# Interleaving the units of the first two token blocks, and giving the eight PSUM banks roles

## The chip, the cores and the metric

One core of a Trainium2 chip runs the whole program. The metric is the device time of one execution in microseconds (us). The core has a matrix engine (TensorE, PE in the profile; its weight loads are PEld), a vector engine (VectorE, DVE), a scalar engine for activations (ScalarE, ACT), a general engine (GpSimd, POOL) and a queue engine that issues most DMA transfers (SyncE, SP). Each engine works through its own instructions strictly in order, and waits on semaphores for the others.

## The reference

Three stages follow one another on 4,608 tokens of 512 features. Only the shapes and the formulas matter here.

```python
# q, k, v: (8 batches, 8 heads, 576, 64)
q_s = softmax(q, axis=-1)            # exp(q - max) / sum, over the 64
k_s = softmax(k, axis=2)             # over the 576 positions
kv  = einsum('bhsd,bhse->bhde', k_s, v)
x   = einsum('bhsd,bhde->bhse', q_s, kv)     # reordered to (4608, 512)

h = x @ w_in                          # (512, 2048)
x = (h * cos(h)) @ w_out              # (2048, 512)

# a token with x @ w_skip > 0 goes through one of 8 experts (argmax of x @ w_gate)
x + gate * (relu(x @ w1[e]) @ w2[e])
```

`w_in` and `w_out` arrive as 64-bit floats, 16.8 MB together, and are turned into 32-bit parts on the chip.

## The kernel before, in words

**Blocks and units.** The tokens are cut into 12 blocks of 384. The hidden width of 2,048 is cut into 16 chunks of 128. A *unit* `n` is one block and one chunk, block = n // 16, chunk = n % 16, so the blocks come one after another. A unit is: `h_mm` (line 318), 12 matmuls of 384 columns into one PSUM bank of the three of pool `ps_h`; the chain `chain_a`, `chain_b`, `chain_c` (lines 326 to 342), which computes h cos(h) by ACT and DVE in turn and splits it into a high and a low part, the low part by POOL (line 342); and `out_mm` (line 344), 9 matmuls of 512 columns into three banks `o0` to `o2`, which collect the output of a block over its 16 chunks. Every product is made of three (high x high, high x low, low x high). The last reader of an `h` bank is the operation of line 335, at the end of `chain_b`.

**The loop.** Iteration n (line 927) issues `h_mm(n)`, then `chain_b(n-1)`, `chain_a(n)`, `chain_c(n-1)`, then `out_mm(n-3)` (LAG is 3). After the last chunk of a block, `evac` (line 356) copies the three `o` banks out: bank 0 and 2 by ACT, bank 1 by DVE (line 361). Between these, numbers in tables say at which chunk other work is issued:

- `attention(j)` makes the input of block j while block j-1 is worked on: `kmax_a`, `kmax_b`, `kmax_c`, `k_exp`, `kv_mm` for a new batch, `q_max`, `q_exp`, `q_norm` for the block's q, then `q_trans` and `x_make`, which leave `xT[j]`, the operand of `h_mm`. `q_max` subtracts on POOL (line 247), `q_norm` multiplies on POOL (line 261). From block 2 on q is transposed by 16 DMAs (`reblock`, line 275) and four DVE operations (`turn`); for blocks 0 and 1 by TensorE.
- `routing(j)` takes the output of block j to the choice of an expert, while block j+1 is worked on.
- `w_step` (line 163): a step turns one 128x512 weight into two 32-bit words (lines 148, 149, 154, 155), finishes the weight of two steps before (lines 143, 152; line 152 on POOL for the weights named in `LOP`, else on DVE), and issues the load of the weight seven steps on. There are 32 weights, two to a chunk. In block 0 the tables `WA`, `WB`, `WC` spread the steps, as every chunk of block 0 needs two new weights.

```python
            w_turn(order[t] if t < len(order) else None, order[t - 2] if 2 <= t < len(order) + 2 else None)
...
            if n < N:
                h_mm(n)
            if 0 <= n - 1 < N:
                chain_b(n - 1)
            if n < N:
                chain_a(n)
            if 0 <= n - 1 < N:
                chain_c(n - 1)
```

**The head and the end.** Before the first unit (lines 873 to 925) come the loads, the attention of block 0 in two halves, the first three weight steps, and matmuls on zeros (`warm`). After the last block come tiles of 256 tokens of one expert (`compute`), at most one tile of 128 (`small`, behind a branch for each of two parities, line 1015), and tiles of 64 (`tiny`, line 676). `tiny` makes all 512 hidden values of a half in one bank `ph`, then four times relu, transpose and copy (lines 697 to 699), then the output matmuls (line 705).

**PSUM.** Eight banks: three `o`, three `h`, two `m` (`misc`, for everything else, among it the attention and the routing).

## Time and profile before

| | |
|---|---|
| three runs | 1260.59, 1261.05, 1454.27 us; median 1261.05 |
| the profiled execution, device time | 1259.9 us |
| its span, first to last recorded event | 1258.1 us |
| mean granted clock of PE | 0.983 of full speed |

The profile is of one execution; its span leaves 1.8 us of the device time outside. A row of a window or a group gives busy time in us and, in brackets, a count of instructions. PEclk is the clock that PE was granted as a share of 2.4 GHz; its lower level is 1.2 GHz. In a group of operations the last part names what ended the idle time before them.

### The profile page before, as it was taken

The page shows a single profiled execution, that of the slowest core. Times are in us where ns is not written, and L with a number is a line of the kernel's source. Part 1 is how long each engine was busy: PE and PEld are TensorE (multiplying, and loading weights), DVE is VectorE, ACT ScalarE, POOL GpSimd, SP SyncE. Part 2 cuts the span into 40 slices and gives each one's busy share as a digit, 9 for nine tenths or more (in the row PEclk, how much of TensorE's full clock was granted, in tenths as well). Part 3 has the DMA queues.
Part 4 walks back from the last instruction along what each step waited for, and adds up shares of the span by engine and source line. Part 5 has one row for each costly group of instructions (what it writes and reads, how often), then busy time and mean ns, then how long its engine had stood idle before and what let it go on. Part 6 is the DMA issues. An engine that isn't in the chain of part 4 may idle for free. (4 is left out here: it accounts for less than half of the span.)

```text
span 1258.1 us, 19774 instructions
## 1 busy us (share of the span) xinstructions
PE 1205.7 (96%) x7012; PEld 1059.3 (84%) x7012; DVE 754.0 (60%) x1508; ACT 719.7 (57%) x1395; POOL 410.8 (33%) x365
## 2 busy tenths in 40 slices
PE   7778999999999999999999999999999999999986
PEld 4657898888898888989988888988888889999974
DVE  7999735556354555635454554535575976776751
ACT  3667655655666565566655566565575545545541
POOL 3666532334324233432423333242120222131121
PEclk8988999999999999999999999999999999999998
DMA  9920222234212223421323232221054677677653
GB/s 301 369 82 1 59 39 68 51 64 111 53 58 44 76 52 64 111 44 49 60 51 79 64 101 35 67 53 25 26 168 160 178 250 230 213 236 229 212 171 107
DMA packets 209493, 138.75 MB, mean 110 GB/s; under 512 B 138200, under 2 KB 173272, under 8 KB 209376
## 3 DMA queue, kind: packets, MB, share of 16 engines
q1 hardware_dynamic: 204272, 125.13, 36.2%
q0 software_dynamic: 5104, 12.17, 2.8%
q8 instruction: 60, 0.98, 0.3%
q14 instruction: 57, 0.47, 0.1%
HBM read 106.35 MB, written 15.95 MB: 97 GB/s over the span
## 5 line engine op out<-in xcount | busy, mean ns | idle before, releaser
L323 PE MATMUL h<-xh,w 128*128 128x384 f32 x1536 | 435.2, 345 | 22.0 <-POOL w L152 6.6
L351 PE MATMUL o<-w,gh 128*128 128x512 f32 x1152 | 364.4, 397 | 2.5 <-ACT x L363 2.5
L323 PEld LDWEIGHTS h<-xh,w 128*128 128x128 f32 x1536 | 283.9, 190 | 39.7 <-DVE w L152 7.7
L342 POOL TENSOR_TENSOR gl<-a,gh 128x384 fp32r<-128x384 f32 x176 | 184.9, 1051 | 395.1 <-ACT gh L340 289.5
L323 PE MATMUL h<-xl,w 128*128 128x384 f32 x768 | 261.4, 340 | 0.1
L351 PEld LDWEIGHTS o<-w,gh 128*128 128x128 f32 x1152 | 215.2, 189 | 39.6 <-ACT x L363 4.1
L351 PE MATMUL o<-w,gl 128*128 128x512 f32 x576 | 229.5, 399 | 1.6 <-POOL gl L342 1.6
L335 DVE SCALAR_TENSOR_TENSOR a<-a,h 128x384 f32<-128x384 f32 x192 | 104.6, 545 | 191.9 <-ACT a L334 191.9
L328 ACT ACTIVATE a<-h 128x384 f32<-128x384 f32 x192 | 93.1, 485 | 182.0 <-PE h L323 107.8
L329 DVE SCALAR_TENSOR_TENSOR a<-a,h 128x384 f32<-128x384 f32 x192 | 105.3, 549 | 140.0 <-ACT a L328 139.9
L323 PEld LDWEIGHTS h<-xl,w 128*128 128x128 f32 x768 | 146.0, 190 | 5.6 <-DVE xl L314 0.7
L340 ACT CAST gh<-a 128x384 fp32r<-128x384 f32 x192 | 97.9, 510 | 72.4 <-DVE a L335 72.4
L844 PE MATMUL h<-xh,w 128*128 128x256 f32 x704 | 137.5, 280 | 0.3 <-DVE w L123 0.3
L351 PEld LDWEIGHTS o<-w,gl 128*128 128x128 f32 x576 | 108.9, 189 | 29.6 <-POOL gl L342 2.8
L123 DVE TENSOR_TENSOR w<-wr,w 128x512 fp32r<-128x512 f32 x192 | 123.9, 687 | 8.1 <-ACT w L122 2.5
L844 PEld LDWEIGHTS h<-xh,w 128*128 128x128 f32 x704 | 113.3, 189 | 4.1 <-ACT w L122 0.7
L855 PE MATMUL o<-w,gh 128*128 128x512 f32 x352 | 112.9, 401 | 0.0
L122 ACT CAST w<-wr 128x512 fp32r<-128x512 f32 x192 | 108.7, 619 | 1.9 <-DMA wr<-in_w 1.9
L333 ACT ACTIVATE a<-a 128x384 f32<-128x384 f32 x192 | 100.8, 525 | 11.0 <-DVE a L329 10.7
L334 ACT ACTIVATE a<-a 128x384 f32<-128x384 f32 x192 | 100.8, 525 | 6.1
L847 ACT ACTIVATE gh<-h 128x256 fp32r<-128x256 f32 x88 | 33.7, 384 | 120.3 <-PE h L844 96.7
L844 PE MATMUL h<-xl,w 128*128 128x256 f32 x352 | 98.7, 280 | 0.0
(220 smaller groups left out, 1470.7 us busy)
## 6 DMA issues: line engine op xcount, KB each, us to landing
wr<-in_w SPq DMA_DIRECT2D x101, 512.0 KB, 4.4
qt<-in_q SPq DMA_DIRECT2D x12, 768.0 KB, 6.7
out<-x SPq DMA_DIRECT2D x36, 256.0 KB, 2.2
wr<-in_w_in SPq DMA_DIRECT2D x16, 512.0 KB, 9.9
wr<-in_w_out SPq DMA_DIRECT2D x16, 512.0 KB, 11.1
xl<-x SPq DMA_DIRECT2D x160, 48.0 KB, 2.1
xh<-qt SPq DMA_DIRECT2D x160, 48.0 KB, 2.1
vt<-in_v SPq DMA_DIRECT2D x7, 1040.0 KB, 6.5
```

The lines of the kernel that those rows point to most:

```text
L122: nc.scalar.copy(hi, src)
L123: nc.vector.tensor_tensor(lo, src, hi.bitcast(F32), op=ALU.subtract)
L323: nc.tensor.matmul(Hp[n], win(a, kk, c), xT[j][b][:, kk, :], start=t == 0, stop=t == len(seq) - 1)
L329: nc.vector.scalar_tensor_tensor(a, a, MAGIC, Hp[n], op0=ALU.subtract, op1=ALU.subtract)
L333: nc.scalar.activation(a, a, AF.Sin, scale=PI)
L334: nc.scalar.activation(a, a, AF.Square)
L335: nc.vector.scalar_tensor_tensor(a, a, 0.5, Hp.pop(n), op0=ALU.subtract, op1=ALU.mult)
L340: nc.scalar.copy(G[n]["h"], a)
L342: eng.tensor_tensor(G[n]["l"], a, G[n]["h"].bitcast(F32), op=ALU.subtract)
L351: nc.tensor.matmul(O[j][g], gg[a][:, g * P:(g + 1) * P], wout(b, c), start=c == 0 and t == 0, stop=c == NC - 1 and t == 2)
L844: nc.tensor.matmul(ps, win2(a, kk, c0, c * P, P), xt[b][:, kk, 0:T2], start=t == 0, stop=t == len(seq) - 1)
L855: nc.tensor.matmul(o[g], g_[a][:, g * P:(g + 1) * P], wout(b, c0 + c), start=c == 0 and t == 0, stop=c == NF - 1 and t == 2)
```

## The change

The units no longer come block by block. A list `UNITS` gives first the chunks 0 to 5 of block 0 (HEAD is 6), then in turn a chunk of block 1 and one of block 0 until block 0 ends (unit 25), then the last six of block 1 (units 26 to 31), then the other blocks as before. The attention of block 1 (`attention_head`) is issued within the iterations 0 to 5, that of block 2 within 8 to 30. The weight steps are one or two an iteration (`WS`), then one, so that they last until iteration 25.

While both blocks are open, both need three `o` banks; so one pool holds all eight banks, and `roles` says which are `o`, `h` and `m`: 3, 3 and 2 up to unit 5, then 3 (block 0) and 3 (block 1) with two `h` and no `m` from unit 6, and again 3, 3 and 2 when block 0 has left its banks, in iteration 28.

The order up to the first unit is another one, with `warm` in portions of four. The subtraction of `q_max` and half of the multiplication of `q_norm` move from POOL to DVE for blocks 0 and 1. The routing of block 0 moves into block 2, beside that of block 1, and its transposition from 16 DMAs and DVE to TensorE (`x2_trans`). `tiny` works in two halves of 256 hidden values with a bank each, and the two branches of `small` change places.

```diff
-WA = (1, 1, 0, 1, 0, 0, 0, 0, 0, 1, 1, 1, 1, 1, 1, 0)
...
+HEAD = 6
+UNITS = [(0, c) for c in range(HEAD)]
+for _c in range(NC - HEAD):
+    UNITS += [(1, _c), (0, HEAD + _c)]
+UNITS += [(1, _c) for _c in range(NC - HEAD, NC)]
+UNITS += [(_j, _c) for _j in range(2, NB) for _c in range(NC)]
...
+KQ = 12, 2, 2
+WS = (1, 1, 2, 2, 2, 2, 2)
...
-    ps_o = m1.enter_context(tc.tile_pool(name="ps_o", bufs=1, space=PSUM))
-    ps_h = m1.enter_context(tc.tile_pool(name="ps_h", bufs=3, space=PSUM))
-    ps_m = m1.enter_context(tc.tile_pool(name="ps_m", bufs=2, space=PSUM))
+    pp = m1.enter_context(tc.tile_pool(name="pp", bufs=1, space=PSUM))
+    banks, used = {}, {"h": 0, "m": 0}
+    def turn_of(kind):
+        used[kind] += 1
+        return bank(banks[kind][used[kind] % len(banks[kind])])
+    roles((0, 1, 2), (3, 4, 5), (6, 7))
...
     def q_max(j, part=None):
...
+            eng = nc.gpsimd if j > 1 else nc.vector
+            eng.tensor_tensor(t, t, st.pop("qm")[:, :, None].to_broadcast([P, NG * H, D]), op=ALU.subtract)
...
+            eng = nc.gpsimd if j > 1 or i else nc.vector
+            eng.tensor_tensor(qt[j][:, :, r, :], qt[j][:, :, r, :],
...
     def attention_head():
+        for c in range(1, 5):
+            add(0, kmax_a, 1, 0, NP, (c,))
+        add(0, q_max, 1)
+        add(1, kmax_b, 1)
+        add(1, x_new, 1)
+        add(1, kmax_c, 1)
+        add(2, q_exp, 1)
+        add(2, k_exp, 1)
+        add(3, q_norm, 1)
+        add(3, kv_mm, 1)
+        for t in range(2):
+            for i in (2 * t, 2 * t + 1):
+                add(4, q_trans, 1, i)
+            for i in (2 * t, 2 * t + 1):
+                add(4 + t, x_make, 1, i)
+        add(KQ[0] - 4, load_q, 2)
+        add(KQ[0], q_max, 2)
+        add(KQ[0] + 1, q_exp, 2)
+        add(KQ[0] + 2, q_norm, 2)
+        add(KQ[0] + 4, q_block, 2)
+        add(KQ[0] + 8, q_turn, 2)
+        add(LAST0, x_new, 2)
+        at = LAST0 + LAG
+        for i in range(NP):
+            add(at + i // 2, q_trans, 2, i)
+            add(at + 1 + i // 2, x_make, 2, i)
+        add(at + 2, x2_trans, 0, 0)
...
-            ph = ps_h.tile([P, DM], F32, tag="h", name="h")
+            ph = [hidden()[:, 0:HM] for v in range(2)]
+            for v, kk in [(0, 0), (1, 0)] + [(v, kk) for v in range(2) for kk in range(1, KD)]:
...
-            for c in range(KD):
-                r = slice(c * P, (c + 1) * P)
-                nc.scalar.activation(a[:, r], ph[:, r], AF.Relu)
-                nc.tensor.transpose(pt[:, r], a[:, r], ident)
-                nc.vector.tensor_copy(g[:, r], pt[:, r])
+            for v in range(2):
+                nc.scalar.activation(a, ph[v], AF.Relu)
+                for c in range(2):
+                    nc.tensor.transpose(pt[:, c * P:(c + 1) * P], a[:, c * P:(c + 1) * P], ident)
+                nc.vector.tensor_copy(g[:, v * HM:(v + 1) * HM], pt)
...
+            if n == POS[1, 0]:
+                roles((5, 6, 7), (3, 4), ())
...
+                if co == NC - 1:
+                    evac(jo, xp)
+                    if jo == 0:
+                        roles((5, 6, 7), (3, 4, 0), (1, 2))
+            if at[0] < len(order) + 2:
+                w_step(WS[n] if n < len(WS) else 1)
...
-        for par, cnt in enumerate((n0, n1) if NE % 2 == 0 else (n1, n0)):
+        for par, cnt in ((1, n1 if NE % 2 == 0 else n0), (0, n0 if NE % 2 == 0 else n1)):
```

**DVE, around `kmax_a`.** The DVE order before, from the chain of units 4 and 5 on; `a` is the chain's tile, `u`, `wr`, `w` belong to the weight step, `km` to the maximum over k.

```order
L335 SCALAR_TENSOR_TENSOR a<-a,h 128x384
L329 SCALAR_TENSOR_TENSOR a<-a,h 128x384
L149 TENSOR_SCALAR u<-wr 128x512
L154 SCALAR_TENSOR_TENSOR wr<-wr,u 128x512
L200 TENSOR_TENSOR km<-kt 128x512
L200 TENSOR_TENSOR km<-km,kt 128x512 x2
L335 SCALAR_TENSOR_TENSOR a<-a,h 128x384
L329 SCALAR_TENSOR_TENSOR a<-a,h 128x384
L149 TENSOR_SCALAR u<-wr 128x512
```

The same engine after the change, from the first chain of unit 0 on; `b_...` is a PSUM bank, `qt` the block's q.

```order
L367 SCALAR_TENSOR_TENSOR a<-a,b_355 128x384
L170 TENSOR_SCALAR u<-wr 128x512
L175 SCALAR_TENSOR_TENSOR wr<-wr,u 128x512
L226 TENSOR_TENSOR km<-kt 128x512
L226 TENSOR_TENSOR km<-km,kt 128x512 x2
L226 TENSOR_TENSOR km<-km,kt 64x512
L274 TENSOR_REDUCE qm<-qt 128x24
L277 TENSOR_TENSOR qt<-qt,qm 128x1536
L373 SCALAR_TENSOR_TENSOR a<-a,b_355 128x384
L367 SCALAR_TENSOR_TENSOR a<-a,b_395 128x384
L170 TENSOR_SCALAR u<-wr 128x512
L173 TENSOR_TENSOR w<-u,w 128x512
```

The maximum over block 1's k starts four units earlier and stands in one piece, and the maximum of q and the subtraction (`qt<-qt,qm`) follow it on DVE.

**PE, two units.** The PE order before, from the last matmul of unit 32 to the first two of unit 33; `h_...` are tiles of the pool of three.

```order
L323 MATMUL h_1970<-xh_1401,w_347 128x384
L351 MATMUL o0_1442<-w_1216,gh_1879 128x512 x2
L351 MATMUL o0_1442<-w_1216,gl_1880 128x512
L351 MATMUL o1_1443<-w_1216,gh_1879 128x512 x2
L351 MATMUL o1_1443<-w_1216,gl_1880 128x512
L351 MATMUL o2_1444<-w_1216,gh_1879 128x512 x2
L351 MATMUL o2_1444<-w_1216,gl_1880 128x512
L323 MATMUL h_2006<-xh_1401,w_385 128x384
L323 MATMUL h_2006<-xl_1402,w_385 128x384
```

After the change, from the last matmul of unit 28 to the first two of unit 29; `b4` is PSUM bank 4, `b0` to `b2` are block 0's output.

```order
L361 MATMUL b4_1714<-xh_435,w_1259 128x384
L389 MATMUL b0_513<-w_1636,gh_1669 128x512 x2
L389 MATMUL b0_513<-w_1636,gl_1670 128x512
L389 MATMUL b1_514<-w_1636,gh_1669 128x512 x2
L389 MATMUL b1_514<-w_1636,gl_1670 128x512
L389 MATMUL b2_515<-w_1636,gh_1669 128x512 x2
L389 MATMUL b2_515<-w_1636,gl_1670 128x512
L361 MATMUL b4_1761<-xh_435,w_1357 128x384
L361 MATMUL b4_1761<-xl_436,w_1357 128x384
```

Unit 29 writes the bank that unit 28 has just written: the list of `h` banks grows from two to three between them, and the turn falls on bank 4 twice.

**PE, one `tiny`.** Before:

```order
L1018 COMPARE_AND_BRANCH
L681 MATMUL m<-ident,tx 128x128 x2
L688 MATMUL h<-wr,a 64x512 x8
L698 MATMUL m<-ident,ta 128x128 x4
L705 MATMUL o<-rv,tg 64x256 x2
L705 MATMUL o<-rx,tg 64x256 x2
L705 MATMUL o<-rv,tg 64x256 x2
L705 MATMUL o<-rx,tg 64x256 x2
L705 MATMUL o<-rv,tg 64x256 x4
L705 MATMUL o<-wr,tg 64x256 x4
```

And after the change, with `b_17806` and `b_17807` the two halves of the hidden values:

```order
L1106 COMPARE_AND_BRANCH
L750 MATMUL b_17801<-ident,tx 128x128 x2
L757 MATMUL b_17806<-wr,a 64x256 x2
L757 MATMUL b_17807<-wr,a 64x256 x2
L757 MATMUL b_17806<-wr,a 64x256 x6
L757 MATMUL b_17807<-wr,a 64x256 x6
L767 MATMUL b_17837<-ident,a 128x128 x2
L767 MATMUL b_17843<-ident,a 128x128 x2
L774 MATMUL b_17847<-rv,tg 64x256 x4
L774 MATMUL b_17847<-rx,tg 64x256 x4
L774 MATMUL b_17847<-rv,tg 64x256 x4
L774 MATMUL b_17847<-wr,tg 64x256 x4
```

The eight matmuls of 512 columns have become sixteen of 256 in two banks, and four transposes in turn have become two pairs.

## Rows read from the trace of the kernel before

**Rows 1.** Page, engines and 40 slices: busy time, then tenths busy per slice

```profile
PE 1205.7 (96%) x7012; PEld 1059.3 (84%) x7012; DVE 754.0 (60%) x1508; ACT 719.7 (57%) x1395; POOL 410.8 (33%) x365
PE   7778999999999999999999999999999999999986
```

**Rows 2.** Windows of DVE-bound and steady stretches: PE, PEld, DVE, ACT, POOL busy, PEclk, DMA

```profile
32.90:66.20 33.30, 21.95 (x99) 18.38 (x98) 31.43 (x42) 18.91 (x39) 21.08 (x17) 0.93 1.06 371
66.20:92.00 25.80, 22.16 (x98) 18.60 (x98) 25.34 (x34) 18.01 (x36) 18.18 (x15) 0.89 0.16 49
92.00:141.50 49.50, 39.73 (x254) 34.52 (x255) 46.58 (x63) 34.88 (x65) 36.06 (x28) 0.90 0.06 17
...
151.10:226.00 74.90, 73.72 (x376) 65.25 (x374) 35.44 (x77) 41.75 (x81) 25.12 (x22) 1.00 0.26 59
...
375.00:447.70 72.70, 72.70 (x373) 64.86 (x372) 35.13 (x77) 41.75 (x80) 24.97 (x22) 1.00 0.27 60
```

**Rows 3.** Waits of PE, 32 to 140 us: total, times, longest

```profile
PE h L323 <- POOL w L152: 6.6, 2, 5.7
PE h L323 <- DVE a L335: 6.0, 3, 2.5
PE h L323 <- DVE w L152: 4.8, 6, 1.4
```

**Rows 4.** Groups of DVE, 20 to 140 us: busy us, mean ns | idle before

```profile
L154 DVE SCALAR_TENSOR_TENSOR wr<-wr,u 128x512 uint32<-128x512 uint32 x32 | 36.8, 1151 | 0.4
L152 DVE TENSOR_TENSOR w<-u,w 128x512 fp32r<-128x512 f32 x20 | 23.5, 1173 | 1.1 <-ACT w L143 0.9
L149 DVE TENSOR_SCALAR u<-wr 128x512 uint32<-128x512 uint32 x32 | 17.0, 531 | 0.0
L329 DVE SCALAR_TENSOR_TENSOR a<-a,h 128x384 f32<-128x384 f32 x16 | 8.7, 543 | 1.3 <-ACT a L328 1.3
...
L216 DVE TENSOR_TENSOR kt<-kt,m 128x2048 f32<-128x2048 f32 x1 | 2.3, 2275 | 0.0
...
L246 DVE TENSOR_REDUCE qm<-qt 128x24 f32<-128x1536 f32 x1 | 1.7, 1740 | 0.0
```

**Rows 5.** Groups of POOL, 20 to 140 us

```profile
L155 POOL TENSOR_TENSOR u<-wr 128x512 uint32<-128x512 uint32 x32 | 38.2, 1196 | 33.3 <-issue 7.8 <-ACT wr L148 6.1 <-DVE wr L154 5.9
...
L247 POOL TENSOR_TENSOR qt<-qt,qm 128x1536 f32<-128x1536 f32 x1 | 2.9, 2869 | 0.5 <-DVE qm L246 0.5
```

**Rows 6.** Timeline of DVE: first weight ready; block 1's middle bank evacuated

```profile
32.24 0.68 DVE L152 TENSOR_TENSOR w<-u,w 128x512 fp32r<-128x512 f32 x1
...
226.01 0.68 DVE L361 TENSOR_SCALAR x<-o 128x512 f32<-128x512 f32 x1
```

**Rows 7.** Timeline of PE, a unit in the steady state

```profile
151.59 0.34 PE L323 MATMUL h<-xh,w 128*128 128x384 f32 x1
...
153.67 0.63 PE L351 MATMUL o<-w,gh 128*128 128x512 f32 x2
...
155.77 0.34 PE L323 MATMUL h<-xh,w 128*128 128x384 f32 x1
```

**Rows 8.** Timeline of ACT, 200 to 202 us

```profile
200.36 1.28 ACT L441 ACT_TABLE_LOAD   x1
201.65 0.22 ACT L441 ACTIVATE sh<-sh 128x24 f32<-128x24 f32 x1
```

**Rows 9.** Groups of ACT, 20 to 140 us: the exponential of q

```profile
L250 ACT ACTIVATE qt<-qt 128x1536 f32<-128x1536 f32 x1 | 1.5, 1485 | 0.0
```

**Rows 10.** Groups of PE, 230 to 300 us: the logits of one block

```profile
L392 PE MATMUL m<-x,wgs 128*32 128x384 f32 x8 | 0.9, 498 | 0.0
```

**Rows 11.** Timeline of PE, the last 36 us of the span

```profile
1222.81 0.55 PE L805 MATMUL h<-w,xh 128*128 128x256 f32 x1 [5.08 <-PEq L1016]
...
1238.74 3.65 PE L688 MATMUL h<-wr,a 128*64 128x512 f32 x16 [0.52 <-ACT a L683]
...
1245.36 0.65 PE L705 MATMUL o<-rv,tg 128*64 128x256 f32 x4
```

More of the change, by code (lines that the diff above doesn't have):

```diff
@@ L295, in q_trans @@
         else:
-            t = (misc() if j else ps_h.tile([P, TB], F32, tag="h", name="h"))[:, 0:TB]
+            t = misc()[:, 0:TB] if j else hidden()
             for g in range(NG):
@@ L316, in body, with h_mm @@
     A, G, Hp, O = {}, {}, {}, {}
-    def h_mm(n):
-        j, c = divmod(n, NC)
-        Hp[n] = ps_h.tile([P, TB], F32, tag="h", name="h")
-        seq = [(a, b, kk) for kk in range(KD) for a, b in (("h", "h"), ("h", "l"), ("l", "h"))]
-        for t, (a, b, kk) in enumerate(seq):
-            nc.tensor.matmul(Hp[n], win(a, kk, c), xT[j][b][:, kk, :],
-                             start=t == 0, stop=t == len(seq) - 1)
+    def h_mm(n, k0=0, k1=KD):
+        j, c = UNITS[n]
+        if k0 == 0:
+            Hp[n] = hidden()
+        for kk in range(k0, k1):
+            for t, (a, b) in enumerate((("h", "h"), ("h", "l"), ("l", "h"))):
+                nc.tensor.matmul(Hp[n], win(a, kk, c), xT[j][b][:, kk, :],
+                                 start=kk == 0 and t == 0, stop=kk == KD - 1 and t == 2)
     def chain_a(n):
@@ L340, in chain_c @@
         nc.scalar.copy(G[n]["h"], a)
-        eng = nc.gpsimd if n < (NB - 1) * NC else nc.vector
+        eng = nc.gpsimd if UNITS[n][0] < NB - 1 else nc.vector
         eng.tensor_tensor(G[n]["l"], a, G[n]["h"].bitcast(F32), op=ALU.subtract)
     def out_mm(n):
-        j, c = divmod(n, NC)
+        j, c = UNITS[n]
         if c == 0:
-            O[j] = [ps_o.tile([P, DM], F32, tag=f"o{g}", name=f"o{g}") for g in range(NG)]
+            O[j] = [acc(g) for g in range(NG)]
         gg = G.pop(n)
@@ L465, in routing @@
         else:
-            for g in range(NG):
+            for g in range(NG if j else 0):
                 add(g, x2_trans, j, g)
@@ L481, in attention @@
         add = lambda s, fn, *a: f.setdefault(s, []).append((fn, a))
-        one = j == 1
-        at = A1 if one else AT
+        at = AT
         add(at[6], q_exp, j)
@@ L493, in attention, with attention_head @@
         add(at[7], q_norm, j)
-        if not one:
-            add(QB, q_block, j)
-            add(QT, q_turn, j)
+        add(QB, q_block, j)
+        add(QT, q_turn, j)
         for i in range(NP):
-            add((Q1 if one else QTR)[i], q_trans, j, i)
-            add((X1 if one else XM)[i], x_make, j, i)
+            add(QTR[i], q_trans, j, i)
+            add(XM[i], x_make, j, i)
+        return f
+    def attention_head():
+        f = {}
+        add = lambda s, fn, *a: f.setdefault(s, []).append((fn, a))
+        for c in range(1, 5):
[25 more added lines that the diff above has]
+        add(at + 2, x2_trans, 0, 0)
         return f
@@ L836, in compute @@
             c0, xt = i % 2 * NF, XH[i % 2]
-            o = [ps_o.tile([P, DM], F32, tag=f"o{(G2 * i + g) % NG}", name="o") for g in range(G2)]
+            o = [acc((G2 * i + g) % NG) for g in range(G2)]
             gg = {}
             def hstep(c):
-                ps = ps_h.tile([P, TB], F32, tag="h", name="h")[:, 0:T2]
+                ps = hidden()[:, 0:T2]
                 seq = [(a, b, kk) for kk in range(KD) for a, b in (("h", "h"), ("h", "l"), ("l", "h"))]
@@ L934, in body @@
                     prefetch, compute, small, small_ids, room, ready, tiny = mlp(mp)
-                r = routing(j - 1, rp, (3, 4, 5, 6, 7, 8, 9, 10, 11, 12) if j == NB - 1 else RT) if 0 < j < NB else {}
-            if j == 0 and FP[c] == 0:
-                run(f.pop(c, []))
-            if n < N:
+                r = routing(j - 1, rp, (3, 4, 5, 6, 7, 8, 9, 10, 11, 12) if j == NB - 1 else RT) if j < NB else {}
+                if j == 2:
+                    early0 = routing(0, rp, (0, 1, 2, 2, 3, 4, 5, 6, 7, 8))
+                    early0[0] = [(x2_trans, (0, 1))]
+                    early0[1] = [(x2_trans, (0, 2))]
+                    for t in early0:
+                        r[t] = early0[t] + r.get(t, [])
+            key = n if j < 2 else c
+            if 0 < n < N:
                 h_mm(n)
```

179 lines of the change are left out of this document (98 added, 81 removed).

## The prediction

> **What bounds the kernel now.** I read the page first. PE is busy for 96% of the span, and its slices are full (9) from the fifth to the thirty-eighth; only the first four and the last two show gaps [rows 1]. So a change of order can win something only in the first 150 us or so and in the last 40. Next the windows by stage [rows 2]. Between 32.9 us, when the first weight is ready [rows 6], and 141.5 us DVE is busy 31.43 + 25.34 + 46.58 = 103.35 of 108.6 us, 95%, while PE is busy 83.84, part of it at a reduced clock (0.89 to 0.93). In block 1 (151.1 to 226.0) DVE is busy 35.44 of 74.90 and PE 73.72. So block 0 is bound by DVE and every later block by PE. Third, the waits of PE in that stretch: it waits for converted weights, from POOL (6.6) and DVE (4.8), and for the end of the chain, `DVE a`, which stands in the same queue behind weight steps (6.0) [rows 3]. Fourth, what fills DVE: the three operations of the weight steps take 36.8 + 23.5 + 17.0 = 77.3 us [rows 4]; one of them takes 0.68 us when nothing disturbs it [rows 6], against a mean of 1.173 for its line [rows 4].
>
> The change does not take this DVE work away. It puts PE work of block 1 beside the later weight steps, at the price of placing block 1's attention, also DVE work, in front of it. The question is when unit 6 starts, and whether PE then runs without gaps. I follow one mark: the copy of block 1's middle output bank, at 226.01 us before [rows 6]. At that point all 32 units of two blocks and the `h_mm` of three more are done, in both orders.
>
> **The change part by part.**
>
> *Up to the first weight.* The loads and operations change places; DVE takes over a subtraction and half of a multiplication, POOL loses them, the first table load of ACT moves ahead of the data. I keep 32.9 us, with 3 us either way, as the operations on the way are the same ones.
>
> *Iterations 0 to 5.* From there until `xT[1]` is complete DVE has, by its order: eleven operations of the kind of line 154, ten of 149 and seven of 152, so 11 x 1.151 + 10 x 0.531 + 7 x 1.173 = 26.2 us; eleven chain operations at 0.543, 6.0; three operations of block 0's last `x_make`, 1.6; and block 1's attention [rows 4]. In the trace of before that attention is sixteen groups of DVE, of which the longest is 2.3 us and the maximum of q 1.7; together 19.9. To them come the subtraction and half of the multiplication. DVE never did these in the trace. The nearest rows are the 128x2048 subtraction of 2.3 us on DVE, which by length gives 1.7 for 128x1536, and the 2.9 us that POOL took for the very same operation [rows 4, 5]; I take 1.8 and, for the half, 0.9. Sum: 26.2 + 6.0 + 1.6 + 22.6 = 56.4. Operations overlap by a few hundredths of a microsecond and DVE idles a little; in the stretch before, the two cancelled, so I add durations and nothing else. Unit 6 can start at 32.9 + 56.4 + 0.5 (the chain that frees its bank) = 89.8 us. The lower bound takes the operations at their undisturbed length, some 10 us less; the upper adds five round trips to PE and ACT, in which DVE waits, of 1.5 us each, 8 more. Attention that the old order spread over block 0 is finished by then, and fewer units are: the new order is behind at this point and must win it back.
>
> At this place stands a rule of the Trainium skill that speaks against the move from POOL to DVE. What the rows show is a 0.68 us operation that lasts 1.173 in the mean while POOL is busy 21.08 of 33.3 us [rows 2, 4, 6]. The page "SBUF — State Buffer", section "SBUF: two separate sides", says that DVE and GpSimd share one pair of ports as an exclusive lock: a DVE operation with two SBUF inputs and a GpSimd operation shut each other out for the whole instruction. The stretched mean agrees with it. By the rule POOL would stand still for the 2.7 us that DVE now takes, and the sum would come out up to 2.7 us later.
>
> *Iterations 6 to 34.* A unit on PE is 2.08 + 2.10 us at full clock [rows 7]. In block 4, which has no new batch of k, 16 units take 72.7 us [rows 2]; without its routing (0.9 for the logits [rows 10] and about as much in small matmuls) and its `x_make` (12 matmuls of 384 columns, as long as one `h_mm`, 2.1) that is 4.3 a unit. So 29 x 4.3 = 124.7 us, with 121 and 127 as bounds. Does DVE keep up? In an iteration with one weight step it has 2 x 0.543 + 0.531 + 1.151 and in eleven of nineteen 1.173, 3.45 in the mean: 80% of 4.3. It does, but not by much.
>
> *Two `h` banks.* In iterations 6 to 28 `h_mm(n+2)` waits until the chain of unit n has left the bank. From the end of `h_mm(n)` PE has two `out_mm` and one `h_mm` to do, 6.3 us. The chain is three ACT operations and two on DVE, 2.6 us (estimate from 0.543 each), and the weight step stands in the queue within it, 2.4 in the mean: 5.0, with 1.3 to spare. Four times something longer is queued behind: the maximum of q (1.7), the exponential of q with a table load on either side, 1.28 + 1.5 + 1.28 [rows 8, 9], `q_norm` and the four turns, about 2 each. Each costs what it exceeds the slack by: 0.4 + 2.8 + 0.7 + 0.7, about 4 us in all. Bounds 0 (the slack is larger, if the steps run undisturbed) and 10 (half a microsecond in each of twenty iterations). Here the Trainium skill has a price that is higher: in the rows the first operation after a table load starts 0.01 us after it ends [rows 8]; "ScalarE: Activation LUTs", section "What ACT_TABLE_LOAD costs", adds a drain of 1.38 us to each switch, which would make the stall 2.8 us longer. The row shows none, and the sum goes by the row.
>
> *Unit 29* takes the bank of unit 28 and has only one `out_mm` between. Block 0's copies and the splits of q stand in front of the end of that chain; I count about 5.8 us against 2.1: a stall of 3.7, once. Block 2's `x_make` and the first `x2_trans`, 2.7 us, stand in this stretch too.
>
> The mark then falls at 89.8 + 124.7 + 4 + 3.7 + 2.7 = 224.9 us, 1.1 earlier than before.
>
> *Block 2* gets block 0's routing. Its small matmuls, 1.7 us, stood before the mark in the old order and are not in my sum for the new one; two more transpose groups are estimated at 0.6 each. That is 2.9 us later on PE (1.7 to 5). What it adds on ACT and DVE is hidden in a block in which DVE is busy less than half of the time [rows 2].
>
> *The end.* In `tiny` the hidden matmuls run from 1238.74 for 3.65 us, and the output matmuls start at 1245.36 [rows 11]: 2.97 us of relu, transpose and copy, four times in turn. In the new order the first half's relu lies beside the second half's matmuls, so one pair of transposes and one copy remain, about 1 us: 2 us won (0.5 to 2.5). The tile of 128 starts after a gap of 5.08 us whose releaser is PE's own queue at the branch of line 1016 [rows 11]: the code of the tile not taken is jumped over. In the new order the tile that is taken stands first, and the jump comes behind it. I take 1.5 us won there (0 to 2.5).
>
> *Sum.* -1.1 + 2.9 - 3.5 = -1.7. The execution of 1259.9 us becomes 1258.2; it lies 1.15 under the median of the runs shown, 1261.05. A measurement of this kernel can tell about 2%, 25 us, from no change.
>
> **The rivals.**
>
> *DVE runs less disturbed.* The means of [rows 4] hold the mutual blocking of before. In iterations 0 to 5 POOL has fewer operations (no q work but half a multiplication, few low parts). With the weight operations near 0.68 and the maximum over k unstretched the stretch is 12 us shorter: 1246. For it: the 0.68 of [rows 6]. Against it: the weight steps come in pairs there, and POOL's addition of 1.196 [rows 5] follows every one of them.
>
> *Two banks bind.* If what stands in the queue between the chain's operations exceeds 3.6 us instead of 2.4 (three stretched operations in every step), each of the twenty iterations of the paired stretch is late by a microsecond: 20 us, 1278, slower than before. The point from which it decides is 6.3 us from the end of `h_mm(n)` to the end of the chain. For it: the 6.0 us that PE waited for `DVE a` with three banks [rows 3]. Against it: then DVE had two steps an iteration.
>
> *The loads come late.* The load of block 2's q waits until block 1's q has been read, at about 85 us, and eight weight loads stand behind it in SP's queue. The first of them is turned in iteration 16, some 45 us later; I see no cost.
>
> **How the numbers follow.** The forecast as worked out, 1250 to 1267: 0.45. DVE less disturbed, around 1246: 0.30. Two banks bind, around 1278: 0.20. Other mishaps: 0.05. A range of 1241 to 1274 takes in the first two cases and the nearer half of the third, and the bounds of the head and the stalls. To be faster by over 2% the time must be below 1235.8; that needs every lower bound at once: 0.03. To be slower by over 2% it must be above 1286.3, beyond the price of the two banks: 0.04. Within 2%: 0.93.
>
> **What would show it.** Right: DVE busy over 90% from 33 to about 90 us; the first matmul of unit 6 near 90; from there PE idle only for a few microseconds in all, the largest piece before unit 29 and a smaller one two units after the exponential of q; the middle bank of block 1 copied near 225; in `tiny` about 1 us between hidden and output matmuls. Wrong: unit 6 before 82 or after 98; waits of PE for the chain (`DVE a`) over 10 us in iterations 6 to 28; or a gain or loss after block 2 other than at the end.

## The result, and the profile after

The changed kernel takes 1276.5 us in the median (four runs, 1276.2 to 1278.7) against 1261.0: a ratio of 1.0129, interval 1.0113 to 1.0145. The prediction was 1258.2, the range 1241 to 1274. It is slower by 1.3%. That is close to the 1278 of the rival "Two banks bind", but by luck: the time was lost in other places, as the experiments show.

Below are PE's row and slices and the granted clock on the page of the profile after, which answer to [rows 1]. The busy time is about the same (1207.8 us against 1205.7), but the first three slices hold less, and the clock is lower in the second and third; the last row is the clock on the page before.

```profile
PE 1207.8 (95%) x7035; PEld 1067.3 (84%) x7036; DVE 754.9 (59%) x1507; ACT 721.8 (57%) x1397; POOL 399.8 (31%) x362
PE   6568899999999999999999999999999999999986
PEclk8678999989999999999999999999999999999998
...
PEclk8988999999999999999999999999999999999998
```

The copies of each block's middle bank cut the span into pieces. Against the kernel before, the mark of block 1 comes 16.1 us later (below, from DVE's timeline, with the copy of block 2 before as the last row; the mark before is 226.01 in [rows 6]), block 2 takes 82.4 us in place of 75.5 (+6.9), blocks 3 to 11 together 2.0 less, and what follows the last block 4.2 less: 16.1 + 6.9 - 2.0 - 4.2 = 16.8, which but for rounding is the difference of the spans (1274.8 - 1258.1 = 16.7).

```profile
242.09 0.69 DVE L399 TENSOR_SCALAR x<-b 128x512 f32<-128x512 f32 x1 [0.27 <-PE b L389]
...
324.48 0.68 DVE L399 TENSOR_SCALAR x<-b 128x512 f32<-128x512 f32 x1
...
301.55 0.68 DVE L361 TENSOR_SCALAR x<-o 128x512 f32<-128x512 f32 x1
```

**The first six units.** The window from the first weight to unit 6 shows DVE (third number) busy for 49.55 of 67.45 us, with PE at a clock of 0.74. It was to be over 90%.

```profile
32.90:100.35 67.45, 39.34 (x223) 33.20 (x223) 49.55 (x67) 32.93 (x59) 24.42 (x20) 0.74 0.53 185
```

DVE's waits there (total, times, longest) are for ACT and PE: in the chain (lines 367 and 373), in `x_make` (351) and in `kmax_c` (242). The longest, 4.8 us, is in the chain while ACT works on the exponentials of q and k. PE's waits in turn are for DVE, and for ACT's part of a weight:

```profile
DVE a L373 <- ACT a L372: 5.8, 3, 4.8
DVE a L367 <- ACT a L366: 4.2, 3, 2.1
DVE xl L351 <- ACT xh L350: 3.2, 3, 1.7
DVE kt L242 <- PE b L240: 2.2, 1, 2.2
```

```profile
PE b L347 <- DVE ql L144: 8.1, 1, 8.1
PE b L240 <- DVE kmx L234: 6.7, 1, 6.7
PE b L361 <- ACT w L164: 3.7, 2, 2.6
```

**Three stalls of PE for the end of a chain.** PE's timeline at the start of units 6 and 29 and in block 2; the row at 107.03 is an undisturbed unit, for comparison:

```profile
100.35 0.69 PE L361 MATMUL b<-xh,w 128*128 128x384 f32 x1 [4.47 <-DVE a L373]
100.84 0.52 PE L361 MATMUL b<-xl,w 128*128 128x384 f32 x1
101.16 0.84 PE L361 MATMUL b<-xh,w 128*128 128x384 f32 x2
...
107.03 0.34 PE L361 MATMUL b<-xh,w 128*128 128x384 f32 x1
107.20 0.34 PE L361 MATMUL b<-xl,w 128*128 128x384 f32 x1
...
211.43 0.69 PE L361 MATMUL b<-xh,w 128*128 128x384 f32 x1 [3.06 <-DVE a L373]
...
273.55 0.69 PE L361 MATMUL b<-xh,w 128*128 128x384 f32 x1 [2.81 <-DVE a L373]
```

Each of these three stalls costs twice. Behind the first, successive matmuls start 0.32 us apart (100.84, 101.16) and not 0.17 to 0.18: the clock is at its lower level, 1.2 GHz, after PE has idled. `h_mm` and `out_mm` behind the first stall take 6.7 us in place of 4.2 (107.03 - 100.35; a unit later it is 4.2); behind the second 1.65 us more than undisturbed, behind the third 2.9. So 10.3 us of waiting took 17.4.

Not every stall of this length does so. At 154.87 PE had waited 2.86 us for the low part of a weight, made on POOL, and in the window around it the granted clock (third number from the end) is 1.00:

```profile
150.00:160.00 10.00, 7.14 (x37) 6.22 (x36) 7.75 (x9) 5.68 (x13) 8.47 (x7) 1.00 0.35 50
```

**The end.** PE's timeline over the small experts answers to [rows 11]; the last two rows are of the kernel before:

```profile
1242.14 0.45 PE L874 MATMUL b<-w,xh 128*128 128x256 f32 x1 [3.51 <-DVEq L1096]
...
1257.13 0.41 PE L750 MATMUL b<-ident,tx 128*128 128x128 f32 x2 [1.00 <-DVEq L1104]
1258.05 3.67 PE L757 MATMUL b<-wr,a 128*64 128x256 f32 x32 [0.52 <-ACT a L752]
...
1262.64 1.08 PE L774 MATMUL b<-rv,tg 128*64 128x256 f32 x8
1263.55 1.03 PE L774 MATMUL b<-rx,tg 128*64 128x256 f32 x8
...
1246.45 1.07 PE L705 MATMUL o<-rv,tg 128*64 128x256 f32 x4
1247.31 1.07 PE L705 MATMUL o<-rx,tg 128*64 128x256 f32 x4
```

The gap ahead of the tile of 128 is 3.51 us in place of 5.08, and from the end of the hidden matmuls (1258.05 + 3.67) to the first output matmul it is 0.92 us in place of 2.97. Two things more stand in these rows. Behind the tile of 128 PE now waits 1.00 us ahead of `tiny`, where before it went on at once: a part of the gap has moved behind the tile. And eight output matmuls take 0.91 us (1262.64 to 1263.55), where before four took 0.86 (1246.45 to 1247.31): behind the four waits of the old `tiny` the granted clock was 0.68 over the output matmuls, now it is 1.00, and all of them take 3.67 us in place of 5.35.

### The profile page after: what moved, and what is told of

Same layout as the page of the kernel before. It is cut to its first block, busy times and chain, and to the rows that moved or that the text cites. A ratio compares the mean times of both kernels' runs of the same rounds, so it can differ in the third digit from the quotient of the medians.

```text
span 1274.8 us, 19797 instructions
## 1 busy us (share of the span) xinstructions
PE 1207.8 (95%) x7035; PEld 1067.3 (84%) x7036; DVE 754.9 (59%) x1507; ACT 721.8 (57%) x1397; POOL 399.8 (31%) x362
## 5 line engine op out<-in xcount | busy, mean ns | idle before, releaser
L361 PE MATMUL b<-xh,w 128*128 128x384 f32 x1536 | 440.3, 348 | 19.5 <-DVE a L373 12.2
L389 PE MATMUL b<-w,gh 128*128 128x512 f32 x1152 | 364.5, 397 | 5.4 <-POOL w L173 4.5
L361 PEld LDWEIGHTS b<-xh,w 128*128 128x128 f32 x1536 | 288.2, 193 | 36.1 <-DVE a L373 14.1
L361 PE MATMUL b<-xl,w 128*128 128x384 f32 x768 | 263.8, 344 | 0.2 <-DVE xl L351 0.2
L389 PEld LDWEIGHTS b<-w,gh 128*128 128x128 f32 x1152 | 215.7, 189 | 42.9 <-POOL w L173 5.6
L389 PE MATMUL b<-w,gl 128*128 128x512 f32 x576 | 228.6, 397 | 0.0
L373 DVE SCALAR_TENSOR_TENSOR a<-a,b 128x384 f32<-128x384 f32 x192 | 104.8, 546 | 193.7 <-ACT a L372 193.3
L366 ACT ACTIVATE a<-b 128x384 f32<-128x384 f32 x192 | 93.4, 486 | 212.2 <-PE b L361 156.8
L367 DVE SCALAR_TENSOR_TENSOR a<-a,b 128x384 f32<-128x384 f32 x192 | 105.6, 550 | 143.0 <-ACT a L366 142.7
L361 PEld LDWEIGHTS b<-xl,w 128*128 128x128 f32 x768 | 148.2, 193 | 5.2 <-DVE xl L351 0.4
L913 PE MATMUL b<-xh,w 128*128 128x256 f32 x704 | 137.5, 280 | 0.3 <-DVE w L144 0.3
L389 PEld LDWEIGHTS b<-w,gl 128*128 128x128 f32 x576 | 108.9, 189 | 26.5
L913 PEld LDWEIGHTS b<-xh,w 128*128 128x128 f32 x704 | 113.3, 189 | 4.1 <-ACT w L143 0.8
L924 PE MATMUL b<-w,gh 128*128 128x512 f32 x352 | 112.9, 401 | 0.0
L916 ACT ACTIVATE gh<-b 128x256 fp32r<-128x256 f32 x88 | 33.8, 384 | 120.7 <-PE b L913 97.2
```

The lines of the kernel that those rows point to most:

```text
L361: nc.tensor.matmul(Hp[n], win(a, kk, c), xT[j][b][:, kk, :], start=kk == 0 and t == 0, stop=kk == KD - 1 and t == 2)
L367: nc.vector.scalar_tensor_tensor(a, a, MAGIC, Hp[n], op0=ALU.subtract, op1=ALU.subtract)
L373: nc.vector.scalar_tensor_tensor(a, a, 0.5, Hp.pop(n), op0=ALU.subtract, op1=ALU.mult)
L389: nc.tensor.matmul(O[j][g], gg[a][:, g * P:(g + 1) * P], wout(b, c), start=c == 0 and t == 0, stop=c == NC - 1 and t == 2)
L913: nc.tensor.matmul(ps, win2(a, kk, c0, c * P, P), xt[b][:, kk, 0:T2], start=t == 0, stop=t == len(seq) - 1)
L924: nc.tensor.matmul(o[g], g_[a][:, g * P:(g + 1) * P], wout(b, c0 + c), start=c == 0 and t == 0, stop=c == NF - 1 and t == 2)
```

## The experiments

All times are medians, each with its ratio to runs of the kernel before on the same chip. "Mark" is the copy of block 1's middle bank, "first weight" the end of the operation that completes the first weight (line 173 after the change, line 152 before), both in us of the one profiled execution. Edits are to the changed kernel, if nothing else is said.

| kernel | us | ratio to before (interval) | first weight | mark | block 2 |
| --- | --- | --- | --- | --- | --- |
| the change | 1276.5 | 1.0129 (1.0113-1.0145) | 31.6 | 242.1 | 82.4 |
| tail_alone (before + end) | 1258.2 | 0.9962 (0.9948-0.9975) | 32.8 | 226.2 | 76.6 |
| gate6 | 1274.9 | 1.0096 (1.0082-1.0111) | 29.8 | 240.3 | 82.0 |
| blk2 | 1271.4 | 1.0079 (1.0059-1.0098) | 29.9 | 240.7 | 77.7 |
| banks | 1266.9 | 1.0040 (1.0025-1.0056) | 30.1 | 231.3 | 81.8 |
| spread8 (on banks) | 1267.6 | 1.0041 (1.0024-1.0057) | 31.0 | 236.2 | 82.1 |
| wfirst (on banks) | 1260.9 | 0.9988 (0.9976-1.0000) | 30.0 | 223.5 | 84.6 |
| all1 | 1254.6 | 0.9945 (0.9928-0.9962) | 31.5 | 224.2 | 78.5 |
| qpool (on all1) | 1255.0 | 0.9931 (0.9915-0.9946) | 30.8 | 224.4 | 78.9 |
| wexp (on all1) | 1257.0 | 0.9948 (0.9932-0.9963) | 30.8 | 225.7 | 78.6 |
| lop19 (on all1) | 1250.7 | 0.9901 (0.9884-0.9919) | 30.0 | 221.0 | 78.7 |
| all2 (all1, wexp, lop19) | 1253.7 | 0.9923 (0.9908-0.9939) | 29.9 | 223.3 | 78.3 |

In the kernel before the first weight is ready at 32.9, the mark at 226.0 and block 2 takes 75.5. The edits to the changed kernel alter nothing ahead of the first weight, and still it comes between 29.8 and 31.6: up to 1.8 us of a difference between two marks can come from there. Where it matters, the text also counts from the first weight to the mark.

### The end by itself: tail_alone

```diff
 (the kernel before)
-for f in (0, 4, 1, 5, 2, 3, 6, 7):
+for f in (0, 1, 4, 5, 2, 3, 6, 7):
...
-for par, cnt in enumerate((n0, n1) if NE % 2 == 0 else (n1, n0)):
+for par, cnt in ((1, n1 if NE % 2 == 0 else n0), (0, n0 if NE % 2 == 0 else n1)):
```

and the two halves of `tiny`'s hidden layer, as in the change.

> The kernel before with nothing of the change but its end: the hidden layer of the small experts (tiny) in two halves and the 128-token experts of the odd slot first. Theory (the end is worth what the two traces show, 39.6 us from the last compute to the end before, 35.4 after, and nothing ahead of it is touched): 1257 us, 4 us below the kernel before (1256 to 1258.5). Rival (the 4 us come from the other data or buffers that the end meets after the new order, not from its own edits): 1261, within 1 us of before.

Measured 0.9962, 4.8 us below before (4.0 between the medians). The end is worth about what it was priced at, and it needs nothing of the rest. The trace also shows how far a block's time can be trusted: blocks 2 to 11, which this kernel leaves as they were, differ from before by up to 2.0 us each, block 2 by 1.1.

### The banks of units 6 and 29: banks

```diff
     roles((5, 6, 7), (3, 4), ())
+    used["h"] += 1
...
     roles((5, 6, 7), (3, 4, 0), (1, 2))
+    used["h"] += 2
```

> The changed kernel with the hidden banks' counter moved on by one at unit 6 and by two where bank 0 joins, so that neither unit 6 nor unit 29 takes the bank that the unit before it still holds. Theory (both waits for the chain are this clash; 4.47 us at 100.35 and 3.06 us at 211.43, and behind each TensorE runs at half clock for about 5 us, which costs 2.5 to 3 us more): both idles go, unit 6 starts at 95.9 to 96.5, the mark of block 1 comes 8 to 12 us earlier (230 to 234), the time is 1266 (1263 to 1269). Rival (the two idles only take up what the next unit would wait for, since the chain of unit 5 ends at 99.8 either way): unit 6 earlier by 4 us but unit 7 waits in its place, the mark within 3 us of 242, the time 1274 to 1276.

Measured 1.0040; the mark came 10.8 us earlier (9.3 counted from the first weight), at the theory's value. No edit touches any work: a counter that counts on while the list it indexes changes length gave unit 6 the bank of unit 5, and unit 29 that of unit 28. Unit 6 now starts at 93.80 instead of 100.35 and waits 2.30 us for `xT[1]` within the unit, as PE's timeline of banks shows:

```profile
93.80 0.36 PE L361 MATMUL b<-xh,w 128*128 128x384 f32 x1
...
97.51 0.44 PE L361 MATMUL b<-xl,w 128*128 128x384 f32 x1 [2.30 <-DVE xl L351]
```

The two stalls and the slow matmuls behind them, 4.47 + 2.5 + 3.06 + 1.65 = 11.7 us, less this new wait of 2.30, make 9.4. The rival, that the waits would only move, is out.

### The first six units without the attention: noattn

```diff
-for c in range(1, 5):
-    add(0, kmax_a, 1, 0, NP, (c,))
...
+xT[1] = xT[0]
```

This kernel leaves out block 1's k, v and q, so only the start of unit 6 is read from it.

> The changed kernel without the attention of block 1 in the first six units: nothing of its k, v and q is worked on, and block 1's units read block 0's x. So it tells only when unit 6 starts. Theory (the six iterations are held by round trips of the attention through the engines' queues: VectorE idles 18 us in 33 to 100): unit 6 starts at 64 to 72, more than 25 us earlier than 100.35, though the attention that is left out has only 25 us of VectorE work. Rival (the weight steps, two an iteration, set the pace and the attention only fills gaps): unit 6 at 82 to 92.

Unit 6 started at 77.99, after the same clash of banks; so the attention costs 100.35 - 77.99 = 22.4 us. That lies between the two expectations. It is close to the 22.6 that the prediction had summed for it. What had been priced too low is the rest: without attention and clash unit 6 could start at 77.99 - 4.85 = 73.1 (an estimate), 40.2 us after 32.9 and 42.2 after this run's own first weight at 30.95, where the prediction had 26.2 + 6.0 + 1.6 = 33.8. And there DVE idles (noattn: PE's timeline at unit 6, the window of the stretch, DVE's waits in it, PE's waits for weights):

```profile
77.99 0.69 PE L361 MATMUL b<-xh,w 128*128 128x384 f32 x1 [4.85 <-DVE a L373]
```

```profile
32.90:75.00 42.10, 27.50 (x92) 22.02 (x90) 28.10 (x36) 21.56 (x44) 18.88 (x16) 0.80 0.94 333
```

```profile
DVE a L367 <- ACT a L366: 13.6, 6, 3.1
```

```profile
PE b L361 <- DVE w L173: 5.9, 4, 2.7
PE b L361 <- ACT w L164: 5.7, 4, 2.6
```

DVE worked 28 of 42 us, and 13.6 us it waited in `chain_a`, once in every iteration, for ACT's copy of a unit that PE had not finished. PE was late because it had waited for the weight. The two take turns: on DVE the weight steps that unit n+1 needs stand behind the `chain_a` that needs unit n's matmuls. "PSUM — Partial Sum Buffer" of the Trainium skill, section "Engine vs sequencer instructions", says that the queues of ScalarE, VectorE and GpSimd are strictly first in, first out; by that nothing behind a waiting `chain_a` can start, and the trace agrees.

### Weight steps ahead of the chain: wfirst

```diff
+if n < HEAD:
+    w_step(WS[n])
 if n < N:
     chain_a(n)
```

on top of banks, with the old call left to later iterations.

> The banks kernel (1266.9) with the weight steps of iterations 0 to 5 ahead of the chain of the same unit in program order, no other edit. Theory (the six units are a loop through in-order queues: a weight step stands on VectorE behind the chain that waits for unit n's matmuls, and unit n+1's matmuls wait for that weight step, so TensorE and VectorE take turns; without the attention six units still took 40 us, of which VectorE was busy 28): TensorE works on unit n while VectorE makes the weight of n+1, the mark of block 1 comes 4 to 8 us earlier than 231.3, the time is 1259 to 1263. Rival (each iteration is made of the attention's own chain, and the weight only fills its gaps): mark and time within 2 us of banks'.

Measured 0.9988 and a mark at 223.5, 7.8 us earlier than banks (7.7 from the first weight), as the theory had it. Unit 6 starts 6.8 us earlier, at 86.99, and DVE's wait for `ACT a L366` (3.7 us in banks) is gone from its list, on this window of wfirst:

```profile
32.90:87.00 54.10, 32.55 (x218) 27.86 (x218) 41.97 (x61) 30.39 (x54) 21.60 (x17) 0.78 0.57 197
```

The wait is one part of the gain; another is that DVE's nine operations of line 170 in this stretch take 3.7 us, where in banks they took 6.5. DVE still idles 12.1 of the 54.1 us, in the round trips of the attention (DVE's waits of wfirst; the 4.6 is behind the exponentials):

```profile
DVE a L373 <- ACT a L372: 5.6, 3, 4.6
DVE xl L351 <- ACT xh L350: 3.2, 3, 1.7
```

Block 2 takes 84.6 us in this run, since both waits of the section on block 2 below stand in it (2.8 and 2.5 us).

### Eight units at the start: spread8

```diff
-HEAD = 6
+HEAD = 8
-WS = (1, 1, 2, 2, 2, 2, 2)
+WS = (1, 1, 2, 2, 2, 2, 2, 2, 2)
```

on banks; the attention lies over eight iterations, and the counter of the `h` banks is set to suit.

> The banks kernel with eight units of block 0 at the start in place of six and the attention of block 1 laid over these eight. Theory (in the first units the engines wait for one another, so that two more units and four more weight pieces fit between the attention's steps): unit 8 starts at 97 to 101, that is within 5 us of where unit 6 starts now, and as two units of 4.3 us are then done, the mark of block 1 comes 4 to 8 us earlier than 231.3; time 1259 to 1263. Rival (work adds up: two iterations more at the 6.7 us that six units took without attention): unit 8 starts at 108 to 110, the mark comes 4 to 5 us later, time 1270 to 1272.

The theory was wrong here. Unit 8 started at 105.85, 12.05 us after the start of unit 6 in banks (11.2 from the first weights), and the mark came 4.9 us later (4.0), as the rival said. Unit 8 came earlier than the rival's 108, and the median time stayed with banks' (1267.6, 1266.9), where the rival had 1270 to 1272. The profiled executions took 1272.1 and 1269.3 us, above these medians, so how the later mark goes with an equal time stays open. Two further iterations cost about 6 us each, not much less than noattn's six did (40.2 / 6 = 6.7): a longer stretch does not loosen a loop in which each turn waits for the one before. PE's waits for weights in spread8 show it, 8.0 and 7.3 us in five waits each:

```profile
PE b L361 <- ACT w L164: 8.0, 5, 2.7
...
PE b L361 <- DVE w L173: 7.3, 5, 2.2
```

### Block 2: gate6 and blk2

In the changed kernel ACT's timeline ahead of the stall at 273.55 reads:

```profile
260.36 1.28 ACT L479 ACT_TABLE_LOAD   x1
261.65 0.22 ACT L479 ACTIVATE sh<-sh 128x24 f32<-128x24 f32 x1
261.89 1.28 ACT L371 ACT_TABLE_LOAD   x1
...
265.42 1.28 ACT L280 ACT_TABLE_LOAD   x1
266.72 1.49 ACT L280 ACTIVATE qt<-qt 128x1536 f32<-128x1536 f32 x1
268.11 1.90 ACT L247 ACTIVATE kt<-kt 128x2048 f32<-128x2048 f32 x1
```

Routing 0's exponential of 0.22 us brings two table loads of its own, one iteration before the exponentials of q and k, and the chain of the unit between ends late. gate6 lets them share the loads:

```diff
-early0 = routing(0, rp, (0, 1, 2, 2, 3, 4, 5, 6, 7, 8))
+early0 = routing(0, rp, (0, 1, 2, 2, 3, 4, 6, 7, 8, 9))
```

> The changed kernel with one number of a table changed: the gate's exp of block 0 (routing 0) in block 2's iteration 6, where q's and k's exp stand, in place of iteration 5. Theory (block 2's loss is ScalarE: the gate's exp needs the table of exp between two iterations that need sine's, two loads of 1.28 us, so the exps of q and k start 2.8 us later, the chain of unit 37 comes late, TensorE idles 2.81 us at 273.55 and then runs at half clock for about 5 us): the idle at 273.55 goes, the span from the middle bank's evacuation of block 1 to that of block 2 falls from 82.4 to 76.5-78, the time from 1276.5 to 1271 (1270 to 1273). Rival (block 2's 6.9 us are the 20 or so extra matmuls and the 11 us more of VectorE of two routings, wherever they stand): the span stays at 81.5-82.5 and the time within 1 us of the changed kernel's.

The stall at 273 is gone, and next to nothing was won in the block: 82.0 us. The time is 1.6 us lower, and the mark 1.8 us earlier, but so is the first weight (29.8 against 31.6), ahead of which nothing is edited. PE's and SP's timelines of gate6 show what took its place:

```profile
295.03 4.18 PE L257 MATMUL b<-vt,kt 128*64 128x65 f32 x80 [2.35 <-DMA vt<-in_v]
...
279.80 8.96 SPq L306 DMA_DIRECT2D xh<-qt  x10
288.86 0.56 SPq L208 DMA_DIRECT2D vt<-in_v  x1
```

The load of v stands in SP's queue behind the transfers of `q_block`, and PE now reached `kv_mm` at 292.7, before v had landed; the clock granted from 290.3 to 300.3 was 0.83. The late unit had been hiding a late load. blk2 issues it earlier:

```diff
-if (j, c) == (2, 8):
+if (j, c) == (2, 5):
     v_place()
...
-if j > 1 and c == VL and j + 1 < NB:
+if j > 1 and c == (6 if j == 2 else VL) and j + 1 < NB:
```

> The changed kernel with the gate's exp of routing 0 in iteration 6 (as gate6) and block 3's load of v issued in iteration 6 of block 2 in place of 11, so ahead of q's block transfers on SyncE's queue. In gate6 the idle of 2.81 us at 273 had gone, but kv_mm then waited 2.35 us for v at 295, v's load having been issued at 288.9 behind 9 us of q's transfers. Theory (block 2's loss is a stall that moves from one wait to the next, each with half-clock matmuls behind it: the exps, then v): both gone, the span of block 2 from 82.0 to 77 to 78.5, the time 1270 to 1272, 5 us below the changed kernel. Rival (block 2 holds 6 to 7 us more of matmuls and VectorE work, whatever waits): 81 to 82, and a time within 1.5 us of gate6's 1274.9.

Block 2 took 77.7 us, the time 1271.4: the theory's values. What is left of block 0's routing is 77.7 - 75.5 = 2.2 us, known to about 1 us: all1's block 2 took 78.5, and that of tail_alone, without this routing, 76.6.

### Together, and the rest of the prediction's terms: all1, qpool, wexp, lop19, all2

all1 has the edits of banks, wfirst and blk2.

> The edits of banks, wfirst and blk2 together. If they add up, 1266.9 - 5 (block 2) - 6 (weight steps first) = 1256 (1252 to 1260), at or below the kernel before. If the time is set by the same waits in each, no more than the best of them: 1261 to 1264.

They add up: 0.9945, with the mark at 224.2. But the order itself wins nothing: from the first weight to the mark all1 takes 192.8 us, the kernel before 193.1. Of the 5.3 us between their profiles (spans of 1252.8 and 1258.1), 1.5 come ahead of the first weight and 0.3 up to the mark; block 2 loses 3.0; blocks 3 to 11 are 2.8 shorter and the end 3.7.

qpool puts block 1's work on q back on POOL (`eng = nc.gpsimd if j > 0 else nc.vector`, and so for the multiplication).

> all1 with block 1's subtraction of q's maximum (1.76 us on VectorE) and the first half of its norm's multiplication (0.96) on GpSimd, as before the change. Theory of the shared port (a VectorE instruction beside GpSimd work takes 1.5 to 2.65 us in place of 0.42 to 0.68: VectorE loses about as much as it hands over): within 1.5 us of all1. Rival (2.7 us of work off the engine that the first units wait for): 2 to 3 us faster, 1252.

0.9931 against all1's 0.9945: the intervals overlap, and 0.0014 is 1.8 us, so the times alone do not decide against the rival. The marks do, one trace each: qpool's is 0.2 us later (0.8 from the first weight). The 2.7 us that leave DVE win nothing there. How DVE and POOL hold each other up shows in banks, where one operation of 0.42 us took 2.65 beside POOL's subtraction (DVE's and POOL's timelines):

```profile
130.96 2.65 DVE L170 TENSOR_SCALAR u<-wr 128x512 uint32<-128x512 uint32 x1
...
138.38 0.42 DVE L170 TENSOR_SCALAR u<-wr 128x512 uint32<-128x512 uint32 x1
...
130.56 2.77 POOL L277 TENSOR_TENSOR qt<-qt,qm 128x1536 f32<-128x1536 f32 x1
```

This agrees with the exclusive lock on shared ports of "SBUF — State Buffer", section "SBUF: two separate sides", of the Trainium skill. By that rule the move to DVE should have cost up to 2.7 us; undone, it gives back nothing that can be measured.

wexp fills DVE's idle 4.9 us under the exponentials with the next two weight steps (`add(2, w_step, 2)` ahead of `q_exp`, and `WS = (1, 1, 2, 0, 2, 2, 2)`).

> all1 (1254.6) with the two weight steps of iteration 3 moved ahead of the exps of q and k in iteration 2. In all1 VectorE idles 4.9 us there, while ScalarE loads the table of exp, works 4.0 us on the exps and loads sine's back. Theory (the idle is on the loop's path; VectorE's 4.5 us of two weight steps then run under the exps): mark of block 1 3 to 5 us earlier than 224.2, time 1250 to 1252. Rival (ScalarE is the loop there: the steps' four casts of 0.6 to 0.7 us, put ahead of the exps, delay the exps and the chain behind them by what VectorE saves): within 1.5 us of all1.

The rival held: 0.9948, the mark 1.4 us later than all1's (2.0 from the first weight). The table load of the exponentials starts 4.9 us later (58.06 against 53.17): the four casts stand ahead of it, and, which the rival did not name, the first of them had to wait 3.47 us for POOL's part of a weight. PE then waited 4.4 us for k's exponential, and DVE idled nearly as long as before, 4.4 us (ACT's timeline and DVE's waits of wexp):

```profile
55.66 0.62 ACT L164 CAST w<-u 128x512 fp32r<-128x512 f32 x1 [3.47 <-POOL u L176]
...
DVE a L373 <- ACT a L372: 5.5, 3, 4.4
```

lop19 takes one weight's low part from POOL to DVE (`LOP` without 19). In banks, whose stretch is that of all1, PE waits for it, and POOL's timeline shows why: it stands behind both halves of q's multiplication.

```profile
148.96 0.50 PE L389 MATMUL b<-w,gh 128*128 128x512 f32 x1 [2.86 <-POOL w L173]
...
143.20 3.09 POOL L292 TENSOR_TENSOR qt<-qt,qs 128x768 f32<-128x768 f32 x2 [1.08 <-DVE qs L287]
146.25 1.44 POOL L380 TENSOR_TENSOR gl<-a,gh 128x384 fp32r<-128x384 f32 x1
147.65 1.26 POOL L173 TENSOR_TENSOR w<-u,w 128x512 fp32r<-128x512 f32 x1
```

> all1 with the low half of one weight (piece 19, the output weight of column 9 of block 0) made on VectorE in place of GpSimd. In all1 TensorE waits 2.86 us for it at 141.85, since on GpSimd it stands behind the multiplication of q of block 2 by its norm, and the granted clock is lower behind it. Theory (the 2.86 us and what the clock takes after them): 3 to 4.5 us off the mark, time 1250 to 1252. Rival (VectorE is as late, having 26 us of work in the 30 from 110 to 140): the wait stays within 1 us, or moves to the chain, time within 1.5 us of all1.

0.9901, the mark at 221.0, 3.2 us earlier than all1's. Of these, 1.6 us are there before PE reaches this weight, and 1.5 of them already at the first weight; from the first weight to the mark the edit is worth 1.8 us. In place of the 2.86 us PE waits 0.78 for this weight, now from DVE, and 0.26 for a later one from POOL. The clock adds nothing: in all1 it was 1.00 behind the wait, and not lower as the expectation had it. This is the fastest kernel of the study, about 1% below the kernel before.

> all1 with the edits of wexp and lop19 together: if both theories hold, 1254.6 - 4 - 3.5 = 1247 (1245 to 1250), 1.2% below the kernel before; if neither, 1254 to 1256.

0.9923, 1253.7 us: between the two. From the first weight to the mark all2 takes 193.4 us; all1's 192.8 with wexp's loss of 2.0 and lop19's gain of 1.8 make 193.0. The two edits add up, but one of them is a loss.

## Why the prediction was wrong

**Up to the first weight.** Right: the first weight was ready at 31.6 instead of 32.9 (29.8 to 31.6 in all traces with this head), within the 3 us.

**Iterations 0 to 5.** Wrong, and the first failing step: "so I add durations and nothing else". Unit 6 was put at 89.8 and started at 100.35, outside the bound of 98. The sum was itself somewhat high: the operations of the stretch add up to 52.8 us instead of 56.4 (weights 25.3, chain 6.6, x 1.1, attention 19.8), and with their overlaps DVE was busy 49.55. But DVE idled 17.9 us, which the sum had at nothing. In the stretch before the change DVE had been busy 95%, and I carried that over to an order in which the work that fills its waits is gone. Of the 17.9, 4.2 are waits in `chain_a`: the loop shown by noattn and opened by wfirst, where unit 6 starts 6.8 us earlier. Most of the rest are round trips of the attention: 4.8 behind the exponentials, 3.2 in `x_make`, 2.2 in `kmax_c`. The prediction had these only in its upper bound, as five of 1.5 us each, and the chain's one in each iteration nowhere. Two agreements are luck: the attention's term, 22.6, is near the 22.4 us that it costs, though only 19.8 of these are DVE's operations; and in wfirst unit 6 starts 57.0 us after the first weight, where the sum had 56.9, with 12.1 us of idling and shorter operations.

The rival "DVE runs less disturbed" had the durations 12 us shorter; they were 3.6 shorter.

**The clash of banks.** At unit 29 it was foreseen, 3.7 us against 3.06 measured. At unit 6 the same rotation puts the unit on the bank of the one before; the prediction allowed "0.5 (the chain that frees its bank)", and it took 4.47.

**What a stall costs after it ends.** No term stood for it. The three long stalls brought 2.5, 1.65 and 2.9 us of matmuls at the lower clock. "TensorE: Matmul & The Clock Gate" of the Trainium skill, section "Part 1: The HAM clock gate (the "warmup" mystery)", has the clock depend on how busy PE has been; the rows behind these three stalls agree. But the 2.86 us at 154.87 left the clock at 1.00, so such a price does not follow every stall of that length, and no run here shows what decides.

**Two `h` banks and the weights behind unit 6.** From unit 6 to the mark 141.7 us passed, where the prediction had 135.1. Besides the two clashes, the waits for the chain there were 0.84 and 1.02 us, less than the 4 predicted (whose four pieces, 0.4 + 2.8 + 0.7 + 0.7, make 4.6), so the rival "Two banks bind" is out as it was put. Three waits for low parts made on POOL (0.90, 2.86 and 0.70) and one for DVE's (0.94) had no term; lop19 takes most of the largest away.

**Block 2.** The work of the second routing was right: 2.9 predicted, 2.2 left in blk2 and 3.0 in all1. Wrong was "What it adds on ACT and DVE is hidden": the low busy share of DVE said nothing on one iteration in which ACT was busy 9.66 of 10 us (262 to 272). The stall and its clock made 2.81 + 2.9 us.

**The end.** Right in its two terms: 2 and 1.5 us predicted, 2.05 in `tiny` and 1.57 at the branch measured. That the whole is near too, 4.2 in the profiles for the 3.5 predicted, is in part luck. The gap moved behind the tile (1.0) and 1.1 us more behind the last matmul were not foreseen, nor that the output matmuls (1.7) and the tile of 128 (14.0 us in place of 15.0) would run more at the full clock. In tail_alone the tile takes 15.1 us, so its part is not the edit's. `tiny` and the branch were not run apart.

So of 18.4 us between the forecast and the profiled execution (1276.6 - 1258.2), the mark holds 17.2: 4.5 + 6.1 at unit 6 (the clash, and DVE's idling net of what came earlier or shorter), 2.5 and 1.0 for the clock behind it and at unit 29, and about 3 that are left over. This is about what PE waits for weights (5.4) and the chain (1.9) behind unit 6, less the 4 predicted; no run shows it by itself. The remainder is block 2 (+4.0), blocks 3 to 11 (-2.0) and the end (-0.7). With clash, loop and block 2 mended, all1 has its mark at 224.2, where 224.9 was forecast; but its first weight comes 1.5 us earlier than before, and without that the mark is within 0.3 us of where it was.

Blocks 3 to 11 differ by up to 3.6 us each from before, in both directions. The cause was not looked for; tail_alone, which does not touch these blocks, differs by up to 2.0 us in one of them.
